# An mLSTM cell with a leaky-ReLU feed-forward block: the first product wholly in 64-row tiles, and the recurrent state updated in place

## The chip, the cores and the metric

The kernel runs on one core of one Trainium2 chip. The metric is the device time of one execution in microseconds (us). Three executions of the kernel before took 621.53, 621.92 and 622.60 us, median 621.92 us. The profile shown below is of one execution with a span of 621.0 us.

## What is computed

Each of 4 x 8 heads runs an mLSTM cell over 768 steps with head size 40. Its outputs are put side by side into rows of 320, and a two-layer block with a leaky ReLU follows.

```python
# q, k, v, o_gate: (4, 8, 768, 40);  i_gate, f_gate: (4, 8, 768)
for t in range(S):
    m_new = np.maximum(f_gate[:, :, t] + m, i_gate[:, :, t])
    f_stab = np.exp(f_gate[:, :, t] + m - m_new)
    i_stab = np.exp(i_gate[:, :, t] - m_new)
    C = f_stab * C + i_stab * outer(v_t, k_t)        # 40 x 40 a head
    n = f_stab * n + i_stab * k_t
    y[:, :, t] = sigmoid(o_t) * (C @ q_t) / max(|n . q_t|, 1)
x = y.transpose(0, 2, 1, 3).reshape(3072, 320)
h = x @ w_in                                          # 320 x 2048
out = np.maximum(0.01 * h, h) @ w_out                 # 2048 x 320
```

q, k, v and the gates are fp32. The two weight matrices come in as 64-bit floats, and the kernel turns them into fp32 itself.

## The kernel before

The sequence is cut into six chunks of 128 steps. A *cell* is one chunk of one of the four batches, so there are 24 cells; it is worked out in matrix form, with the state C (and n as its 41st column) carried from chunk to chunk. The four cells of a chunk give 512 rows of x, a *group*, and the feed-forward block runs on one group while the cells of the next chunk are worked out in between.

A cell goes through these steps, all named in the profile by the tiles they write. `u_transpose` transposes k and q (tkq, L311), and ScalarE copies them out (kqT, L314). `u_scores` makes the scores (sc, L323): two heads at a time, in the upper and lower half of TensorE's rows, since a head has 40 of 64 padded rows; VectorE multiplies them onto the mask w (L327). `u_state` multiplies the old state with q (pc, L337; VectorE scales it into hn, L341), makes the new contribution to the state (dC, L348), scales the old state on GpSimd (L357), and adds dC on VectorE (L358). The old and the new state lie in two tiles, C0 and C1, which swap from chunk to chunk. `u_values` multiplies w with v (pa, L367), VectorE adds it to hn (L369), forms the denominator, and `gate` makes x (VectorE L385, GpSimd L388). `u_x` transposes x (xt, L399 and L400), and ScalarE copies it into xT (L401, L403). `prep_mask`, `prep_exp`, `prep_vu` and `prep_o` prepare the next cell's mask (GpSimd L279, ScalarE L287), scaled values (GpSimd L295) and output gate (ScalarE L302).

The first product has 320 rows of w_in to contract: two full blocks of 128 and a rest of 64. For a pair of hidden blocks of 128, `full` runs two 128-row matmuls for each of the two blocks (L413), and `close` adds the rest of both in two 64-row matmuls (L419), one in each half of TensorE's rows, into two PSUM banks. For this xT holds the two full blocks, and the rest twice, once in each partition half. ScalarE then applies the leaky ReLU (act, L427). A pair is cut into two *units*: the first block, and the second block with the close. In the first group the pairs are run in halves of 256 columns (`half`, one unit each), so that the first two batches can start early. The second product runs in units of four hidden blocks (`part`, po, L457); ScalarE copies its result out (L462), and a transfer stores it.

Order of work: each engine takes its instructions in the order in which the program lists them (the program turns off reordering for TensorE, VectorE, ScalarE and GpSimd). `first_chunk` writes out by hand the order of the four cells of chunk 0, the first two half units and the conversion of the first weights. After it a loop goes over the units of the feed-forward block of one group and lets the units of the next chunk's cells in between, spread evenly. The conversion of a slice of weights (`narrow_weights`: one ScalarE and six VectorE instructions, L166 to L184) is likewise given out in pieces over the units of the first group. The transfers on SyncE's queue are placed by a planner.

PSUM has two pools of four banks: `mm` for ph (first product), po (second product) and the first masks, `c` for all tiles of the cells.

Of the kernel before, what the change touches and what calls it, by code (L numbers as in the profile page):

```python
# [9 lines left out]
F32 = mybir.dt.float32  # L10
# [3 lines left out]
ALU = mybir.AluOpType  # L14
# [4 lines left out]
def kernel(  # L19
# [26 lines left out]
    nc = tc.nc  # L46
    B, H, S, D = q.shape
    P = 128
    BH = B * H
    NB = S // P  # L50
    NS = B * NB
    Dm, FF = moe_w_in.shape
    PR = H // 2
    DP = 64
    D1 = D + 1
    NF = FF // P
    GT = B * P
    KF = Dm // P
    KR = Dm - KF * P
    assert NB * P == S and NF * P == FF and NF % 4 == 0 and D <= DP and H == 2 * PR and BH <= P  # L60
    assert KR == DP and GT * 4 <= 2048

    consts = ctx.enter_context(tc.tile_pool(name="consts", bufs=1))
    gp = ctx.enter_context(tc.tile_pool(name="gates", bufs=1))
    wk = ctx.enter_context(tc.tile_pool(name="wk", bufs=2))
# [38 lines left out]
        nc.gpsimd.memset(va_t[n][:, :, D:], 1.0)  # L104


    C_t = [consts.tile([P, B, PR, 2, D1], F32, name=f"C{n}") for n in range(2)]
    for t in C_t:
        nc.gpsimd.memset(t[:], 0.0)

    QN = NF // 4
    QC = 4 * P
    WC = KF * QC + 2 * P
    w_in = consts.tile([P, QN, WC], F32, name="w_in")
    w_out = consts.tile([P, NF, Dm], F32, name="w_out")

    def w_full(kk, f):
        n, e = divmod(f, 4)  # L120
        return w_in[:, n, kk * QC + e * P : kk * QC + (e + 1) * P]

    def w_rest(r, j):
        n, e = divmod(j, 2)
        return w_in[KR * r : KR * (r + 1), n, KF * QC + e * P : KF * QC + (e + 1) * P]

    wide = moe_w_in.dtype == U64
    raws = {}
# [1 line left out]
    def load_weights(n):  # L130

        if n < QN:
            dst = w_in[:, n, :]
        else:
            dst = w_out[:, 4 * (n - QN) : 4 * (n - QN + 1), :].rearrange("p a d -> p (a d)")
        to = dst
        if wide:
            raw = wk.tile([P, dst.shape[1]], U64, name="raw", bufs=3)
            raws[n] = (raw, dst)
            to = raw[:]  # L140
        if n < QN:
            cols = slice(n * QC, (n + 1) * QC)
            for kk in range(KF):
                nc.sync.dma_start(to[:, ts(kk, QC)], moe_w_in[ts(kk, P), cols])
            rest = moe_w_in[KF * P :, cols].rearrange("d (j two e) -> two d j e", two=2, e=P)
            for r in range(2):
                nc.sync.dma_start(
                    to[KR * r : KR * (r + 1), KF * QC :].rearrange("p (j e) -> p j e", e=P), rest[r],
                )
        else:  # L150
            rows = moe_w_out[(n - QN) * QC : (n - QN + 1) * QC, :]
            nc.sync.dma_start(to.rearrange("p (a d) -> p a d", d=Dm), rows.rearrange("(a p) d -> p a d", p=P))
# [40 lines left out]
    def gates(c):  # L193


        m0 = m0s.get(c)
        cs = ts(c, P)
        n = P if c == 0 else BH
        fc, il = (f0[:], i0[:]) if c == 0 else (f_sb[:, cs], i_sb[:, cs])
        F = wk.tile([n, P], F32, name="F", bufs=1)  # L200
        nc.vector.tensor_tensor_scan(F[:], fc, zeros[:n], 0.0, op0=ALU.add, op1=ALU.add)
        if c > 0:
            il_t = wk.tile([BH, P], F32, name="il", bufs=1)
            nc.vector.tensor_scalar(il_t[:], il, scalar1=m0[:], scalar2=None, op0=ALU.subtract)
            il = il_t[:]
        m = wk.tile([n, P], F32, name="m", bufs=1)
        nc.vector.tensor_tensor_scan(m[:], fc, il, -1e30 if c == 0 else 0.0, op0=ALU.add, op1=ALU.max)
        a = wk.tile([n, P], F32, name="a")
        nc.vector.tensor_tensor(a[:], F[:], m[:], op=ALU.subtract)
        if c > 0:  # L210
            nc.sync.dma_start(a_dr[c], a[:])
        bu = wk.tile([BH, 3, P], F32, name="bu")
        nc.vector.tensor_tensor(bu[:, 0, :], il[:BH], F[:BH], op=ALU.subtract)
        nc.scalar.activation(bu[:, 1, :], bu[:, 0, :], AF.Exp, bias=a[:BH, P - 1 :], scale=1.0)
        nc.scalar.activation(bu[:, 2, :], a[:BH], AF.Exp)
        if c + 1 < NB:
            m1 = wk.tile([BH, 1], F32, name="m0")
            if c == 0:
                nc.vector.tensor_copy(m1[:], m[:BH, P - 1 :])
            else:  # L220
                nc.vector.tensor_tensor(m1[:], m0[:], m[:, P - 1 :], op=ALU.add)
            m0s[c + 1] = m1
        return bu, a
# [105 lines left out]
    def u_state(s):  # L329
        c, b = divmod(s, B)  # L330
        d = st[s]
        C, C_new = C_t[c % 2], C_t[(c + 1) % 2]
        if c > 0:
            d["hn"] = wk.tile([P, H, D1], F32, name="hn")
            pc = psc.tile([P, H, D1], F32, name="pc", tag="c")
            for j in range(PR):
                nc.tensor.matmul(  # L337
                    pc[:, 2 * j : 2 * j + 2, :].rearrange("p h d -> p (h d)"), lhsT=d["kqT"][:, 1, j, :],
                    rhs=C[:, b, j].rearrange("p h d -> p (h d)"), start=True, stop=True,
                )  # L340
            nc.vector.tensor_tensor(  # L341
                d["hn"][:], pc[:], gT[:, c, 2, ts(b, H)].unsqueeze(2).to_broadcast([P, H, D1]), op=ALU.mult,
            )
        if c + 1 < NB:
            dC = psc.tile([P, PR, D1], F32, name="dC", tag="c")
            for h in range(H):
                rows = slice(DP * (h % 2), DP * (h % 2) + DP)
                nc.tensor.matmul(  # L348
                    dC[rows, h // 2, :], lhsT=d["kq"][:, 0, h, :], rhs=d["vu"][:, h, :], start=True, stop=True,
                )  # L350
            for r in range(2):
                rows = slice(DP * r, DP * r + DP)
                if c == 0:
                    nc.vector.tensor_copy(C_new[rows, b, :, r, :], dC[rows])
                else:
                    g = gL[rows, c, b * H + r : (b + 1) * H : 2].unsqueeze(2).to_broadcast([DP, PR, D1])
                    nc.gpsimd.tensor_tensor(C_new[rows, b, :, r, :], C[rows, b, :, r, :], g, op=ALU.mult)  # L357
                    nc.vector.tensor_tensor(C_new[rows, b, :, r, :], C_new[rows, b, :, r, :], dC[rows], op=ALU.add)  # L358

    def u_values(s):  # L360
        c, b = divmod(s, B)
# [28 lines left out]
    def u_x(s):  # L390

        c, b = divmod(s, B)
        d = st[s]
        if b == 0:
            st["xT", c] = wk.tile([P, KF + 1, GT], F32, name="xT")
        xT = st["xT", c]
        xt = psc.tile([P, KF + 1, P], F32, name="xt", tag="c")
        for kk in range(KF):
            nc.tensor.transpose(xt[:, kk, :], d["x"][:, ts(kk, P)], ident[:])  # L399
        nc.tensor.transpose(xt[:KR, KF, :], d["x"][:, KF * P :], ident[:])  # L400
        nc.scalar.copy(xT[:, :KF, ts(b, P)], xt[:, :KF, :])  # L401
        for r in range(2):
            nc.scalar.copy(xT[KR * r : KR * (r + 1), KF, ts(b, P)], xt[:KR, KF, :])  # L403
        del st[s]


    def ff_units(g):
        xT = st["xT", g]
        acts = {}

        def full(f, ph, cols):
            for kk in range(KF):
                nc.tensor.matmul(  # L413
                    ph[:, cols], lhsT=w_full(kk, f), rhs=xT[:, kk, cols], start=(kk == 0), stop=False,
                )

        def close(j, ph, cols):
            for r in range(2):
                nc.tensor.matmul(  # L419
                    ph[r][:, cols], lhsT=w_rest(r, j), rhs=xT[KR * r : KR * (r + 1), KF, cols],  # L420
                    start=False, stop=True,
                )
            for r in range(2):
                f = 2 * j + r
                if f not in acts:
                    acts[f] = wk.tile([P, GT], F32, name=f"act{f}", bufs=1)
                nc.scalar.activation(acts[f][:, cols], ph[r][:, cols], AF.Prelu, alpha=0.01)  # L427

        def pair(j):
            ph = {}  # L430

            def first():
                ph[0] = psf.tile([P, GT], F32, name="ph0", tag="mm")
                full(2 * j, ph[0], slice(0, GT))

            def second():
                ph[1] = psf.tile([P, GT], F32, name="ph1", tag="mm")
                full(2 * j + 1, ph[1], slice(0, GT))
                close(j, ph, slice(0, GT))

            return [first, second]

        def half(j, h):

            ph = [psf.tile([P, GT], F32, name=f"ph{r}", tag="mm") for r in range(2)]
            cols = ts(h, GT // 2)
            for r in range(2):
                full(2 * j + r, ph[r], cols)
            close(j, ph, cols)

        po = {}

# [201 lines left out]
```

## Time and profile before

| what | value |
|---|---|
| median of three executions | 621.92 us |
| TensorE matmuls (PE) busy | 597.4 us, 96% of the span |
| TensorE weight loads (PEld) busy | 385.7 us, 62% |
| VectorE (DVE) busy | 178.2 us, 29% |
| ScalarE (ACT) busy | 185.7 us, 30% |
| GpSimd (POOL) busy | 111.8 us, 18% |
| second product, L457 | 768 records, 221.4 us busy |
| first product, full tiles, L413 | 448 records, 186.2 us busy |
| first product, 64-row tiles, L419 | 224 records, 57.2 us busy |

How to read it: an fp32 matmul or weight load appears as two records, one for each pass. Matmuls are pipelined and their ends are modelled, so successive ones overlap in the list, and it is their starts that tell the pace. The form of a matmul on the array is written as rows*columns, 128*128 for the full array and 64*128 for a 64-row tile. Where a line of the timeline has [2.46 <-POOL x L388], the engine was idle for 2.46 us before it, until the named instruction released it.

### The profile page before, as it was taken

What the parts mean: (1) busy time and instruction counts of PE and PEld (TensorE: products, weight loads), DVE (VectorE), ACT (ScalarE), POOL (GpSimd) and SP (SyncE); (2) the same over time, 40 slices, a digit from 0 to 9 for tenths busy, and PEclk for the clock granted to TensorE, in tenths of its full rate; (3) what the DMA queues carried; (4) which work ended last, traced back from release to release, by engine and by line L of the source; (5) the groups of instructions that cost most, each with busy time, mean ns of one, the idle gap of its engine ahead of it and who ended that gap; (6) DMA issues with size and microseconds to landing.
All of it is one profiled execution on the core that took longest, in us unless ns stands there. A gap on an engine that the chain in (4) does not pass through costs nothing.

```text
span 621.0 us, 7722 instructions
## 1 busy us (share of the span) xinstructions
PE 597.4 (96%) x3046; PEld 385.7 (62%) x3046; DVE 178.2 (29%) x343; ACT 185.7 (30%) x493; POOL 111.8 (18%) x110
## 2 busy tenths in 40 slices
PE   6986998998999999999999999999999999999997
PEld 5865666776554577654577745577745567743575
DVE  5838656886221121311121411211101111100000
ACT  4442345332334403144403144223043231012100
POOL 3023021554202220302202302202101010000000
PEclk9997999999899999999999999999999999999999
DMA  9999434433221331312321313303300000000000
GB/s 180 226 234 217 147 97 130 91 73 67 67 51 36 76 77 28 81 23 65 77 51 48 78 24 74 77 13 86 77 11 1 1 0 22 11 12 0 0 22 21
DMA packets 111346, 41.50 MB, mean 67 GB/s; under 512 B 101104, under 2 KB 105616, under 8 KB 111312
## 3 DMA queue, kind: packets, MB, share of 16 engines
q1 hardware_dynamic: 111024, 40.79, 29.0%
q8 instruction: 24, 0.39, 0.3%
q10 hardware_dynamic: 288, 0.23, 0.2%
q14 instruction: 10, 0.08, 0.0%
HBM read 37.00 MB, written 4.01 MB: 66 GB/s over the span
## 4 chain that ended last, share of the span: by engine, by line
PE 87%; DVE 5%; SPq 3%; POOL 1%; ACT 1%; issue 1%; DMA 1%; POOLq 0%; DVEq 0%; ACTq 0%
PE po L457 32%; PE ph L413 27%; PE ph L419 8%; PE pa L367 6%; PE sc L323 4%; PE pc L337 3%; PE tkq L311 3%; SPq L242 2%; PE dC L348 2%; POOL x L388 1%; PE xt L399 1%; DMA va<-in_v_dram 1%; DVE hn L369 1%; DVE x L385 1%; DVE w_in L176 0%
## 5 line engine op out<-in xcount | busy, mean ns | idle before, releaser
L457 PE MATMUL po<-w_out,act 128*128 128x320 f32 x768 | 221.4, 440 | 0.0
L413 PE MATMUL ph<-xT,w_in 128*128 128x512 f32 (+1 forms) x448 | 186.2, 552 | 0.4 <-DVE w_in L184 0.4
L457 PEld LDWEIGHTS po<-w_out,act 128*128 128x128 f32 x768 | 142.3, 191 | 55.0 <-issue 1.9
L413 PEld LDWEIGHTS ph<-xT,w_in 128*128 128x128 f32 x448 | 81.5, 195 | 68.8 <-issue 58.5
L427 ACT ACTIVATE act<-ph 128x512 f32<-128x512 f32 (+1 forms) x112 | 53.7, 531 | 151.6 <-PE ph L419 151.6
L388 POOL TENSOR_TENSOR x<-x,den 128x320 f32<-128x320 f32 x24 | 22.9, 955 | 396.6 <-DVE x L385 396.6
L327 DVE TENSOR_TENSOR w<-w,sc 128x512 f32<-128x512 f32 x48 | 30.7, 681 | 182.3 <-PE sc L323 182.3
L287 ACT ACTIVATE w<-w,gT 128x128 f32<-128x128 f32 x192 | 58.7, 397 | 13.0 <-POOL w L279 12.8
L419 PE MATMUL ph<-xT,w_in 64*128 64x512 f32 (+1 forms) x224 | 57.2, 588 | 0.0
L462 ACT COPY y<-po 128x320 f32<-128x320 f32 x24 | 10.2, 424 | 148.5 <-PE po L457 86.6
L367 PEld LDWEIGHTS pa<-va,w 128*128 128x128 f32 x384 | 49.1, 203 | 8.5 <-issue 5.9
L279 POOL TENSOR_TENSOR w<-w,cmask 128x1024 f32<-128x1024 f32 x20 | 50.1, 2503 | 0.0
L367 PE MATMUL pa<-va,w 128*128 128x41 f32 x384 | 49.5, 291 | 0.4 <-DVE w L327 0.4
L314 ACT COPY kqT<-tkq 128x512 f32<-128x512 f32 x48 | 26.1, 593 | 75.2 <-PE tkq L311 75.1
L419 PEld LDWEIGHTS ph<-xT,w_in 64*128 64x128 f32 x224 | 17.3, 189 | 36.3 <-issue 36.3
L323 PEld LDWEIGHTS sc<-kqT 40*128 40x128 f32 x384 | 26.1, 204 | 12.8 <-issue 5.3
L323 PE MATMUL sc<-kqT 40*128 40x128 f32 x384 | 30.4, 302 | 1.7 <-ACT kqT L314 1.7
L369 DVE TENSOR_TENSOR hn<-hn,pa 128x328 f32<-128x328 f32 x20 | 9.9, 496 | 74.9 <-PE pa L367 74.9
L311 PEld LDWEIGHTS tkq<-ident,kq 128*128 128x128 f32 x192 | 23.7, 152 | 10.8 <-issue 9.4
L311 PE MATMUL tkq<-ident,kq 128*128 128x128 f32 x192 | 28.3, 295 | 0.0
L341 DVE TENSOR_TENSOR hn<-pc,gT 128x328 f32<-128x328 f32 x20 | 10.0, 498 | 60.6 <-PE pc L337 60.6
L337 PEld LDWEIGHTS pc<-C,kqT 128*128 128x128 f32 x160 | 20.6, 191 | 7.0 <-issue 5.3
(65 smaller groups left out, 316.8 us busy)
## 6 DMA issues: line engine op xcount, KB each, us to landing
w<-a_dr SPq DMA_DIRECT2D x20, 512.0 KB, 4.9
raw<-in_moe_w_out_dram SPq DMA_DIRECT2D x4, 1280.0 KB, 5.7
raw<-in_moe_w_in_dram SPq DMA_DIRECT2D x8, 512.0 KB, 5.5
kq<-in_k_dram SPq DMA_DIRECT2D x24, 160.0 KB, 3.1
kq<-in_q_dram SPq DMA_DIRECT2D x24, 160.0 KB, 3.5
va<-in_v_dram SPq DMA_DIRECT2D x24, 160.0 KB, 2.8
o_sb<-in_o_gate_dram SPq DMA_DIRECT2D x24, 160.0 KB, 4.7
out_dram<-y SPq DMA_DIRECT2D x24, 160.0 KB, 1.8
```

The lines of the kernel that those rows point to most:

```text
L279: nc.gpsimd.tensor_tensor(w[:], w[:], cmask[:].unsqueeze(1).to_broadcast([P, H, P]), op=ALU.add)
L287: nc.scalar.activation(w[:, h, :], w[:, h, :], AF.Exp, bias=gT[:, c, 0, bh : bh + 1], scale=1.0)
L311: nc.tensor.transpose(tp[:, j, :], d["kq"][:, i, 2 * j : 2 * j + 2, :].rearrange("p h d -> p (h d)"), ident[:],)
L323: nc.tensor.matmul(sc[r][:, j, :], lhsT=kqT[rows, 0, j, :], rhs=kqT[rows, 1, j, :], start=True, stop=True,)
L327: nc.vector.tensor_tensor(w[:, r::2, :], w[:, r::2, :], sc[r][:], op=ALU.mult)
L337: nc.tensor.matmul(pc[:, 2 * j : 2 * j + 2, :].rearrange("p h d -> p (h d)"), lhsT=d["kqT"][:, 1, j, :], rhs=C[:, b, j].rearrange("p h d - ...
L367: nc.tensor.matmul(pa[:, h, :], lhsT=d["w"][:, h, :], rhs=d["va"][:, h, :], start=True, stop=True)
L388: nc.gpsimd.tensor_tensor(x3, x3, d["den"][:].unsqueeze(2).to_broadcast([P, H, D]), op=ALU.mult)
L413: nc.tensor.matmul(ph[:, cols], lhsT=w_full(kk, f), rhs=xT[:, kk, cols], start=(kk == 0), stop=False,)
L419: nc.tensor.matmul(ph[r][:, cols], lhsT=w_rest(r, j), rhs=xT[KR * r : KR * (r + 1), KF, cols], start=False, stop=True,)
L427: nc.scalar.activation(acts[f][:, cols], ph[r][:, cols], AF.Prelu, alpha=0.01)
L457: nc.tensor.matmul(po[n][:], lhsT=acts[f][:, ts(n, P)], rhs=w_out[:, f, :], start=(f == 0), stop=(f == NF - 1),)
```

## The change

The whole first product is put into 64-row tiles. The 320 rows of w_in are five blocks of 64. For a pair of hidden blocks, one takes the upper half of TensorE's rows and the other the lower half: five steps, each of two 64-row matmuls side by side, one for each hidden block, into two banks. Thus no 128-row matmul is left in the first product, and TensorE's form doesn't change within it. Each half of the rows needs all five blocks of x on its own partitions, so xT now holds all of x on both partition halves. The five transposed blocks come out of the transposes on one half each, so the order of blocks differs between the halves (SLOTS), and the first copy still serves both; four smaller copies do the rest. w_in is laid out to match: two hidden blocks' weights for one half, two for the other, five blocks deep.

To make room, the second state tile goes (C is scaled and added to in place), and the small tiles a and bu have one buffer instead of two.

```diff
+    SLOTS = ([0, 2, 4, 1, 3], [1, 3, 0, 2, 4])
...
-    C_t = [consts.tile([P, B, PR, 2, D1], F32, name=f"C{n}") for n in range(2)]
-    for t in C_t:
-        nc.gpsimd.memset(t[:], 0.0)
+    C = consts.tile([P, B, PR, 2, D1], F32, name="C")
+    nc.gpsimd.memset(C[:], 0.0)
...
-            for kk in range(KF):
-                nc.sync.dma_start(to[:, ts(kk, QC)], moe_w_in[ts(kk, P), cols])
-            rest = moe_w_in[KF * P :, cols].rearrange("d (j two e) -> two d j e", two=2, e=P)
             for r in range(2):
...
+                while at < KC:
+                    ks = SLOTS[r][at:]
+                    n_k = next((i for i in range(1, len(ks)) if ks[i] != ks[i - 1] + 2), len(ks))
+                    nc.sync.dma_start(half[:, at : at + n_k, :], src[:, ks[0] : ks[0] + 2 * n_k - 1 : 2, :])
+                    at += n_k
...
-        a = wk.tile([n, P], F32, name="a")
+        a = wk.tile([n, P], F32, name="a", bufs=1)
-        bu = wk.tile([BH, 3, P], F32, name="bu")
+        bu = wk.tile([BH, 3, P], F32, name="bu", bufs=1)
...
-                    nc.gpsimd.tensor_tensor(C_new[rows, b, :, r, :], C[rows, b, :, r, :], g, op=ALU.mult)
-                    nc.vector.tensor_tensor(C_new[rows, b, :, r, :], C_new[rows, b, :, r, :], dC[rows], op=ALU.add)
+                    nc.gpsimd.tensor_tensor(C[rows, b, :, r, :], C[rows, b, :, r, :], g, op=ALU.mult)
+                    nc.vector.tensor_tensor(C[rows, b, :, r, :], C[rows, b, :, r, :], dC[rows], op=ALU.add)
...
-        nc.scalar.copy(xT[:, :KF, ts(b, P)], xt[:, :KF, :])
-        for r in range(2):
-            nc.scalar.copy(xT[KR * r : KR * (r + 1), KF, ts(b, P)], xt[:KR, KF, :])
+        nc.scalar.copy(xT[:, :KF, tok], xt[:, :KF, :])
+        nc.scalar.copy(xT[:DP, KF + 1 :, tok], xt[DP:, :KF, :])
+        nc.scalar.copy(xT[DP:, KF : 2 * KF, tok], xt[:DP, :KF, :])
+        nc.scalar.copy(xT[:DP, KF, tok], xt[:DP, KF, :])
+        nc.scalar.copy(xT[DP:, 2 * KF, tok], xt[:DP, KF, :])
...
-        def full(f, ph, cols):
-            for kk in range(KF):
-                nc.tensor.matmul(
-                    ph[:, cols], lhsT=w_full(kk, f), rhs=xT[:, kk, cols], start=(kk == 0), stop=False,
-                )
...
+        def rows(j, ph, cols, slots):
+            for slot in slots:
+                for r in range(2):
+                    nc.tensor.matmul(
+                        ph[r][:, cols], lhsT=w_row(r, slot, j), rhs=xT[DP * r : DP * (r + 1), slot, cols],
+                        start=(slot == 0), stop=(slot == KC - 1),
+                    )
...
             def first():
-                ph[0] = psf.tile([P, GT], F32, name="ph0", tag="mm")
-                full(2 * j, ph[0], slice(0, GT))
+                ph.extend(psf.tile([P, GT], F32, name=f"ph{r}", tag="mm") for r in range(2))
+                rows(j, ph, slice(0, GT), range(3))
 
             def second():
-                ph[1] = psf.tile([P, GT], F32, name="ph1", tag="mm")
-                full(2 * j + 1, ph[1], slice(0, GT))
-                close(j, ph, slice(0, GT))
+                rows(j, ph, slice(0, GT), range(3, KC))
+                relu(j, ph, slice(0, GT))
```

More of the change, by code (lines that the diff above doesn't have):

```diff
@@ L59 @@
     KR = Dm - KF * P
+    KC = Dm // DP
+    SLOTS = ([0, 2, 4, 1, 3], [1, 3, 0, 2, 4])
     assert NB * P == S and NF * P == FF and NF % 4 == 0 and D <= DP and H == 2 * PR and BH <= P
-    assert KR == DP and GT * 4 <= 2048
+    assert KR == DP and KC == 5 and KC * DP == Dm and GT * 4 <= 2048
     consts = ctx.enter_context(tc.tile_pool(name="consts", bufs=1))
@@ L104, with f_of, w_row @@
         nc.gpsimd.memset(va_t[n][:, :, D:], 1.0)
-    C_t = [consts.tile([P, B, PR, 2, D1], F32, name=f"C{n}") for n in range(2)]
-    for t in C_t:
-        nc.gpsimd.memset(t[:], 0.0)
+    C = consts.tile([P, B, PR, 2, D1], F32, name="C")
+    nc.gpsimd.memset(C[:], 0.0)
     QN = NF // 4
     QC = 4 * P
-    WC = KF * QC + 2 * P
+    WC = KC * 2 * P
     w_in = consts.tile([P, QN, WC], F32, name="w_in")
     w_out = consts.tile([P, NF, Dm], F32, name="w_out")
[L119 to L123, printed above, removed]
+    def f_of(r, j):
         n, e = divmod(j, 2)
-        return w_in[KR * r : KR * (r + 1), n, KF * QC + e * P : KF * QC + (e + 1) * P]
+        return 4 * n + 2 * r + e
+    def w_row(r, slot, j):
+        n, e = divmod(j, 2)
+        at = (2 * slot + e) * P
+        return w_in[DP * r : DP * (r + 1), n, at : at + P]
     wide = moe_w_in.dtype == U64
@@ L141, in load_weights @@
         if n < QN:
-            cols = slice(n * QC, (n + 1) * QC)
-            for kk in range(KF):
-                nc.sync.dma_start(to[:, ts(kk, QC)], moe_w_in[ts(kk, P), cols])
-            rest = moe_w_in[KF * P :, cols].rearrange("d (j two e) -> two d j e", two=2, e=P)
             for r in range(2):
-                nc.sync.dma_start(
-                    to[KR * r : KR * (r + 1), KF * QC :].rearrange("p (j e) -> p j e", e=P), rest[r],
-                )
+                cols = slice(n * QC + 2 * P * r, n * QC + 2 * P * (r + 1))
+                src = moe_w_in[:, cols].rearrange("(k p) c -> p k c", p=DP)
+                half = to[DP * r : DP * (r + 1), :].rearrange("p (k c) -> p k c", k=KC)
+                at = 0
+                while at < KC:
[3 more added lines that the diff above has]
+                    at += n_k
         else:
@@ L331, in u_state @@
         d = st[s]
-        C, C_new = C_t[c % 2], C_t[(c + 1) % 2]
         if c > 0:
@@ L353, in u_state @@
                 if c == 0:
-                    nc.vector.tensor_copy(C_new[rows, b, :, r, :], dC[rows])
+                    nc.vector.tensor_copy(C[rows, b, :, r, :], dC[rows])
                 else:
                     g = gL[rows, c, b * H + r : (b + 1) * H : 2].unsqueeze(2).to_broadcast([DP, PR, D1])
-                    nc.gpsimd.tensor_tensor(C_new[rows, b, :, r, :], C[rows, b, :, r, :], g, op=ALU.mult)
-                    nc.vector.tensor_tensor(C_new[rows, b, :, r, :], C_new[rows, b, :, r, :], dC[rows], op=ALU.add)
+                    nc.gpsimd.tensor_tensor(C[rows, b, :, r, :], C[rows, b, :, r, :], g, op=ALU.mult)
+                    nc.vector.tensor_tensor(C[rows, b, :, r, :], C[rows, b, :, r, :], dC[rows], op=ALU.add)
     def u_values(s):
@@ L394, in u_x @@
         if b == 0:
-            st["xT", c] = wk.tile([P, KF + 1, GT], F32, name="xT")
+            st["xT", c] = wk.tile([P, KC, GT], F32, name="xT")
         xT = st["xT", c]
@@ L400, in u_x @@
         nc.tensor.transpose(xt[:KR, KF, :], d["x"][:, KF * P :], ident[:])
-        nc.scalar.copy(xT[:, :KF, ts(b, P)], xt[:, :KF, :])
-        for r in range(2):
-            nc.scalar.copy(xT[KR * r : KR * (r + 1), KF, ts(b, P)], xt[:KR, KF, :])
+        tok = ts(b, P)
+        nc.scalar.copy(xT[:, :KF, tok], xt[:, :KF, :])
[3 more added lines that the diff above has]
+        nc.scalar.copy(xT[DP:, 2 * KF, tok], xt[:DP, KF, :])
         del st[s]
@@ L409, in ff_units, with relu @@
         acts = {}
-        def full(f, ph, cols):
-            for kk in range(KF):
-                nc.tensor.matmul(
-                    ph[:, cols], lhsT=w_full(kk, f), rhs=xT[:, kk, cols], start=(kk == 0), stop=False,
-                )
-        def close(j, ph, cols):
-            for r in range(2):
[L419 to L424, printed above, removed]
+        def rows(j, ph, cols, slots):
[5 more added lines that the diff above has]
+                    )
+        def relu(j, ph, cols):
+            for r in range(2):
+                f = f_of(r, j)
                 if f not in acts:
@@ L429, in pair @@
         def pair(j):
-            ph = {}
+            ph = []
             def first():
-                ph[0] = psf.tile([P, GT], F32, name="ph0", tag="mm")
-                full(2 * j, ph[0], slice(0, GT))
+                ph.extend(psf.tile([P, GT], F32, name=f"ph{r}", tag="mm") for r in range(2))
+                rows(j, ph, slice(0, GT), range(3))
             def second():
-                ph[1] = psf.tile([P, GT], F32, name="ph1", tag="mm")
-                full(2 * j + 1, ph[1], slice(0, GT))
-                close(j, ph, slice(0, GT))
+                rows(j, ph, slice(0, GT), range(3, KC))
+                relu(j, ph, slice(0, GT))
             return [first, second]
@@ L446, in half @@
             cols = ts(h, GT // 2)
-            for r in range(2):
-                full(2 * j + r, ph[r], cols)
-            close(j, ph, cols)
+            rows(j, ph, cols, range(KC))
+            relu(j, ph, cols)
         po = {}
```

## The prediction

> **What bounds the kernel now.** I read the busy shares first, then the chain of work that ended last:
>
> ```profile
> PE 597.4 (96%) x3046; PEld 385.7 (62%) x3046; DVE 178.2 (29%) x343; ACT 185.7 (30%) x493; POOL 111.8 (18%) x110
> ...
> PE 87%; DVE 5%; SPq 3%; POOL 1%; ACT 1%; issue 1%; DMA 1%; POOLq 0%; DVEq 0%; ACTq 0%
> ```
>
> TensorE (PE) is busy for 96% of the span and makes up 87% of the chain. All that its instructions waited for from 160 us to the end, in the view of waits, is:
>
> ```profile
> PE xt L399 <- POOL x L388: 1.0, 4, 0.3
> ```
>
> So after 160 us only what TensorE does back to back counts. Before 160 us it had 23.6 us without a running matmul (60 + 60 + 80 us less 45.6 + 57.9 + 77.1 busy), and there the other engines count too.
>
> A busy TensorE is not a streaming TensorE. The timeline of the last group, which has no cell work in it (columns: start us, duration us, what):
>
> ```profile
> 545.66 3.60 PE L413 MATMUL ph<-xT,w_in 128*128 128x512 f32 x8
> 549.18 1.13 PE L419 MATMUL ph<-xT,w_in 64*128 64x512 f32 x4
> 550.25 3.70 PE L413 MATMUL ph<-xT,w_in 128*128 128x512 f32 x8
> 553.88 1.13 PE L419 MATMUL ph<-xT,w_in 64*128 64x512 f32 x4
> 554.93 3.70 PE L413 MATMUL ph<-xT,w_in 128*128 128x512 f32 x8
> ```
>
> An fp32 matmul shows as two passes, so x8 is four full matmuls, and x4 is two 64-row matmuls that run side by side as two pass times. Starts count, since the ends are modelled and overlap. One round lasts 554.93 - 550.25 = 4.68 us. What should a pass cost? The weight loads of a full stream tell:
>
> ```profile
> 401.49 0.19 PEld L413 LDWEIGHTS ph<-xT,w_in 128*128 128x128 f32 x1 [0.24 <-issue]
> 401.92 0.19 PEld L413 LDWEIGHTS ph<-xT,w_in 128*128 128x128 f32 x1 [0.24 <-issue]
> ```
>
> They come every 0.43 us, each beside a running pass. The round is 8 + 2 = 10 pass times, 4.29 us at 0.429. The other 0.39 us is the price of going into the 64-row form and back: about 0.20 us per change of form. It splits. Eight full passes take 549.18 - 545.66 = 3.52 us when full tiles precede, and 553.88 - 550.25 = 3.63 us after a 64-row tile: about 0.10 us is the first weight load, which nothing covers. The rest of 0.20 (3.52 less 8 x 0.429 is 0.09) is the array running empty before the form changes.
>
> **What the Trainium skill says.** "TensorEngine Tiling (Array Packing)", Key Properties: changing the tiling mode, not just the tile, drains TensorE; tiles of one mode work independently. The trace agrees: 0.09 us ahead of the first 64-row pass, and scores (L323) that run in pairs. "TensorE: Matmul & The Clock Gate", The mechanism: a weight load overlaps running matmuls only when the row group differs. Read strictly that would leave loads of one tile exposed; the full stream above has each load beside a pass, so here the measurement decides. Its part on the HAM clock gate says that the clock falls to half after about 3.4 us without work. The trace half agrees: after an idle 2.46 us before 155.16 the granted clock averaged 0.66 over 155 to 160 us, that is 3.4 us at half, or 1.7 us lost; after 1.66 us it stayed:
>
> ```profile
> 90.00:100.00 10.00, 8.34 (x64) 6.43 (x66) 7.11 (x13) 6.50 (x20) 0.00 (x0) 1.00 0.50 149
> 155.00:160.00 5.00, 4.84 (x14) 3.31 (x15) 3.84 (x5) 1.19 (x4) 4.17 (x5) 0.66 0.46 125
> ...
> 94.99 1.23 PE L323 MATMUL sc<-kqT 40*128 40x128 f32 x16 [1.66 <-ACT kqT L314]
> 155.16 0.44 PE L399 MATMUL xt<-ident,x 128*128 128x128 f32 x2 [2.46 <-POOL x L388]
> ```
>
> **The change part by part.** *Streaming.* A pair of hidden blocks was 8 full passes and 2 paired ones; it becomes 10 paired ones. The work in passes is the same, if a long run of pairs keeps 0.429 us a pass. Two places of the trace bear on that:
>
> ```profile
> 192.74 1.13 PE L419 MATMUL ph<-xT,w_in 64*128 64x512 f32 x4
> 193.70 1.06 PE L323 MATMUL sc<-kqT 40*128 40x128 f32 x16
> ...
> 34.16 2.08 PE L323 MATMUL sc<-kqT 40*128 40x128 f32 x16
> 36.17 0.69 PE L399 MATMUL xt<-ident,x 128*128 128x128 f32 x2
> ```
>
> A closing pair followed by scores, also in 64-row form, takes 193.70 - 192.74 = 0.96 us: 0.53 for the first pass with its bare load, 0.43 for the second, nothing for a change. Eight score pairs of 128 columns at the half clock take 2.01 us, of which 8 x 0.213 = 1.71 is streaming and about 0.3 the change at both ends: no extra per pair. So I take 0.429. Bounds: 0.429 and 0.53 (each load bare). The weight loads grow from 6 to 10 fp32 loads a pair, two at a time, each hidden under a pass.
>
> *Changes of form.* I counted them in the order in which TensorE receives its instructions (the column-tiled dC counts as a form too): 200 before, 155 after. By group of 512 tokens: 64 to 41 in the first, 32 to 30 in each of the next three, 24 to 22 in the fifth, 16 to 2 in the last. A change between long matmuls costs 0.20 us. Beside cell work it costs less: starts in the trace give 0.12 before or after pa, 0.16 before tkq or pc, 0.13 before xt, because those are short and their loads were never wholly hidden. In a middle group 13 changes go (8 into the closing pair, 2 back to full tiles, 1 to scores, 2 from scores), 13 x 0.20 = 2.6 us, and 11 come (po to ph, three tkq to ph and one xt to ph at 0.20; two pa to ph at 0.12; one more each to tkq, pc, pa, xt, 0.57 together), 1.8 us. Net 0.8 us, four times: 3.1 us. Last group: 14 x 0.20 = 2.8 us, all on the path.
>
> *First group.* Its 23 fewer changes are worth 4.6 us by the same prices, but not all is on the path. The first two half units (from 38 us) feed a stretch that ends in TensorE waiting 4.98 us for x at 57.8 us: nothing gained. The eight half units from 59.2 us to the gate transposes at 81.7 us run back to back: 15 changes, 3.0 us. From there to the scores at 95.0 us TensorE waits: masks' exp on ScalarE, w_out's conversion and the next gates on VectorE and then kqT make a chain of 13.3 us that does not shrink; the idle 1.66 us before those scores grows to about 3. Then two more halves save 0.6 us. So 3.6 us, less a possible half-clock spell after the longer gap, 0 or 1.7 us; I take the middle, 0.8.
>
> *ScalarE.* Per cell, two 64 x 256 copies more:
>
> ```profile
> 34.27 0.37 ACT L401 COPY xT<-xt 128x256 f32<-128x256 f32 x1 [3.24 <-PE xt L400]
> 34.54 0.53 ACT L403 COPY xT<-xt 64x128 f32<-64x128 f32 x2
> ```
>
> By the spacing, 0.27 to 0.37 us each, so 0.55 to 0.74 us a cell, 13 to 18 us in all on an engine that is 30% busy. Queued behind are a mask's exp, a prelu or kqT. The first matmul of a group follows the last transposes of x by 24 matmul records of po (253.55 to 260.01 us): hidden. In the first group the first half unit starts some 0.4 us later, inside the slack before 57.8 us. The prelu of a pair is due a whole pair (4.3 us) later, since four banks hold two pairs: hidden.
>
> *State in place.* GpSimd's scaling (L357, two of 0.58 us, up to 2.25 us together beside VectorE) now waits for pc's matmuls to have read C; before it ran ahead. VectorE's two adds follow it, about 1 us later than now; behind them stands hn += pa, which waits for matmuls at least one unit (1.7 us) later. TensorE wants dC's bank two allocations on. Cost: 0, at most 0.6 us a cell, 20 cells. One memset (1.19 us) goes from idle GpSimd: 0.
>
> *Loads and buffers.* w_in moves the same bytes in as many transfers, 2 KB rows instead of 4 KB and 1 KB. ScalarE never waited for w_in's landing: 0. One buffer for a and bu: the first a is read by matmuls whose results VectorE uses before the next gates; each later one by a transfer a group earlier: 0.
>
> Sum: 3.1 + 2.8 + 3.6 - 0.8 = 8.7 us; 621.9 - 8.7 = **613.2 us**.
>
> **Rivals.** *The start keeps its time*: the gain before 160 us is eaten by ScalarE and VectorE there and a half-clock spell comes on top: 621.9 - 5.9 = 616.0, or 617.7. For it: the waits before 160 us. Against: eight halves stand in a row without a wait. *Loads are bare in the paired stream*: 0.104 us on each of 400 passes, 41.6 us, and some 10 in the first group: about 665 us, slower. For it: the only in-pair step of L419 is 0.53 us. Against: it follows a change; the scores show none. *New waits take the place*: 0.65 us for each of 20 cells by the later state and copies, 13 us: 626 us, slower. For it: both are in the cell's own path. Against: 1.0 us of waits after 160 us, with units of 1.7 us and more between the steps.
>
> **How the numbers follow.** Forecast 0.75, start keeps its time 0.16, bare loads 0.04, new waits 0.05. The range 610 to 617.5 takes in first-group gains from nothing to 5 us, with or without a half-clock spell, and leaves out the two slower cases and the far end of the first rival. Faster 0.75 + 0.16 less a little for part of the new waits: 0.90; same 0.02; slower 0.08.
>
> **What would show it.** Right: in the last group a stream of 64-row passes every 0.429 us, 8 rounds from 545.66 to 583.08 (37.4 us) becoming 34.6 us; 96.3 us from 163.70 to 260.01 becoming 95.5; the wait for kqT before the first scores of the second chunk at about 3 us. Wrong: passes further apart than 0.44 us, new TensorE waits for ScalarE's xT or act after 160 us, GpSimd's C ending after the next pa, or a long half-clock stretch.

## The result, and the profile after

The changed kernel takes 615.36 us (median, 614.92 to 615.85) beside 622.26 us (621.53 to 622.95): the ratio is 0.989, 95% interval 0.9876 to 0.9904, or 6.9 us less. Measured again later (e8), it took 615.07 us beside 622.69 us, ratio 0.988 (0.9863 to 0.9896). The forecast was 613.2 us with a range of 610.0 to 617.5.

The profiled span fell by 7.5 us, from 621.0 to 613.5 us. The busy shares and the chain of work, in the page of the changed kernel:

```profile
PE 584.0 (95%) x3494; PEld 390.2 (64%) x3494; DVE 177.1 (29%) x343; ACT 206.1 (34%) x541; POOL 107.4 (18%) x109
PE 79%; SPq 7%; DVE 4%; DMA 3%; ACT 3%; POOL 2%; issue 2%; POOLq 0%; DVEq 0%; ACTq 0%
```

TensorE has 448 records more (1120 in the first product for 672), and is busy for 13.4 us less. ScalarE is busy for 20.4 us more: the five copies per cell into xT, where three were, make 17.5 us of it (38.8 for 21.3). What is not TensorE's in the chain lies before 160 us, where it now follows transfers (SPq, DMA); no engine shows a wait for the landing of w_in, so the page alone does not say that they cost time. All that TensorE waited for after 160 us, in the view of waits:

```profile
PE xt L402 <- POOL x L391: 0.9, 4, 0.3
```

It is the same short wait as before (1.0 us), so no new one came up behind 160 us. The last group's first product, eight pairs, in the timeline (start us, duration us):

```profile
541.03 34.60 PE L420 MATMUL ph<-xT,w_in 64*128 64x512 f32 x160
575.57 1.61 PE L457 MATMUL po<-w_out,act 128*128 128x320 f32 x5
```

From 541.03 to 575.57 it takes 34.54 us, where it took 37.42 us (545.66 to 583.08). The weight loads in that stream:

```profile
541.03 0.30 PEld L420 LDWEIGHTS ph<-xT,w_in 64*128 64x128 f32 x4 [0.44 <-issue]
541.57 0.19 PEld L420 LDWEIGHTS ph<-xT,w_in 64*128 64x128 f32 x2 [0.23 <-issue]
542.00 0.19 PEld L420 LDWEIGHTS ph<-xT,w_in 64*128 64x128 f32 x2 [0.24 <-issue]
542.43 0.19 PEld L420 LDWEIGHTS ph<-xT,w_in 64*128 64x128 f32 x2 [0.24 <-issue]
```

Loads now come two at a time, one for each half of the rows, every 0.43 us: the pace of a pass is what it was in full tiles. Only the first step, from 541.03 to 541.57, is longer by the bare load.

Where the 7.5 us came from, by the starts of the groups' first products in both timelines:

| stretch (from one profile each) | before, us | after, us | gain, us | forecast, us |
|---|---|---|---|---|
| to the second group's first product | 163.70 | 161.74 | 1.96 | 2.8 |
| second to fourth group, each | 96.31 | 95.67 | 0.64 | 0.8 |
| fifth group | 93.01 | 92.28 | 0.73 | 0.8 |
| last group's first product | 37.42 | 34.54 | 2.88 | 2.8 |

Behind the first group these times come again within 0.03 us in every profile of the same code; the first row does not, as the experiments show.

### The profile page after: what moved, and what is told of

Its sections match the earlier page's. It is cut to its first block, busy times and chain, and to the rows that moved or that the text cites. A ratio compares the mean times of both kernels' runs of the same rounds, so it can differ in the third digit from the quotient of the medians.

```text
span 613.5 us, 8662 instructions
## 1 busy us (share of the span) xinstructions
PE 584.0 (95%) x3494; PEld 390.2 (64%) x3494; DVE 177.1 (29%) x343; ACT 206.1 (34%) x541; POOL 107.4 (18%) x109
## 4 chain that ended last, share of the span: by engine, by line
PE 79%; SPq 7%; DVE 4%; DMA 3%; ACT 3%; POOL 2%; issue 2%; POOLq 0%; DVEq 0%; ACTq 0%
PE po L457 31%; PE ph L420 30%; PE pa L370 6%; SPq L246 4%; PE sc L327 3%; PE pc L340 3%; PE tkq L315 3%; SPq L152 2%; PE dC L351 2%; DMA va<-in_v_dram 1%; DMA raw<-in_moe_w_in_dram 1%; PE xt L402 1%; ACT w L291 1%; POOL w L283 1%; POOL x L391 1%
## 5 line engine op out<-in xcount | busy, mean ns | idle before, releaser
L420 PE MATMUL ph<-xT,w_in 64*128 64x512 f32 (+1 forms) x1120 | 224.1, 546 | 1.1 <-ACT xT L405 0.6
L420 PEld LDWEIGHTS ph<-xT,w_in 64*128 64x128 f32 x1120 | 107.1, 192 | 85.4 <-issue 78.3
L370 PEld LDWEIGHTS pa<-va,w 128*128 128x128 f32 x384 | 48.8, 202 | 13.4 <-issue 6.7
L360 POOL TENSOR_TENSOR C<-C,gL 64x164 f32<-64x164 f32 x32 | 14.8, 462 | 184.9 <-PE pc L340 183.7
L327 PE MATMUL sc<-kqT 40*128 40x128 f32 x384 | 28.1, 287 | 2.7 <-ACT kqT L318 2.7
L299 POOL TENSOR_TENSOR vu<-va,gT 128x328 f32<-128x328 f32 x20 | 18.8, 941 | 28.0 <-issue 18.8
```

The lines of the kernel that those rows point to most:

```text
L327: nc.tensor.matmul(sc[r][:, j, :], lhsT=kqT[rows, 0, j, :], rhs=kqT[rows, 1, j, :], start=True, stop=True,)
L370: nc.tensor.matmul(pa[:, h, :], lhsT=d["w"][:, h, :], rhs=d["va"][:, h, :], start=True, stop=True)
L420: nc.tensor.matmul(ph[r][:, cols], lhsT=w_row(r, slot, j), rhs=xT[DP * r : DP * (r + 1), slot, cols], start=(slot == 0), stop=(slot == KC ...
```

## The experiments

### The state alone (e1)

```diff
-    C_t = [consts.tile([P, B, PR, 2, D1], F32, name=f"C{n}") for n in range(2)]
...
+    C = consts.tile([P, B, PR, 2, D1], F32, name="C")
...
-        a = wk.tile([n, P], F32, name="a")
+        a = wk.tile([n, P], F32, name="a", bufs=1)
...
-                    nc.gpsimd.tensor_tensor(C_new[rows, b, :, r, :], C[rows, b, :, r, :], g, op=ALU.mult)
...
+                    nc.gpsimd.tensor_tensor(C[rows, b, :, r, :], C[rows, b, :, r, :], g, op=ALU.mult)
...
```

> The kernel before with only the state updated in place and one buffer for a and bu; the first product as before. My theory (the wait of GpSimd for pc is hidden): 621.9 us, within 0.5 us of the kernel before, and no new TensorE wait. Rival (the later state costs part of the gain): 2 to 12 us slower, with VectorE's adds or pa later in every cell.

Measured: 622.61 beside 622.37 us, ratio 1.0003 (0.9994 to 1.0012). The later scaling of the state is hidden, and the rival falls. One part of the expectation was not met: the profile has TensorE waits of 4.5 us together before pa, all ahead of 160 us, where the profile before has 0.4. They are not the state's, since e9, with both state tiles, shows 4.4 us of them.

### The copies alone (e2)

```diff
+        x2 = wk.tile([P, KF, P], F32, name="x2", bufs=1)
+        nc.scalar.copy(x2[:DP], xt[DP:, :KF, :])
+        nc.scalar.copy(x2[DP:], xt[:DP, :KF, :])
```

> The kernel before with two more 64 x 256 copies of the transposed x per cell on ScalarE, into a tile that nothing reads. My theory: hidden but for the first group, where the bank is given back later: two waits of dC of about 0.3 us, so 0 to 0.8 us slower than the kernel before. Rival (ScalarE's copies hold TensorE up in every group): 24 cells by 0.5 us, some 12 us slower.

Measured: 623.94 beside 622.37 us, ratio 1.0026 (1.0017 to 1.0034), or 1.6 us slower (1.1 to 2.1). This is far from 12 us, and more than my 0 to 0.8. Two places show in its timeline:

```profile
38.62 3.78 PE L416 MATMUL ph<-xT,w_in 128*128 128x256 f32 x8 [0.52 <-ACT xT L401]
58.28 0.69 PE L399 MATMUL xt<-ident,x 128*128 128x128 f32 x2 [4.97 <-POOL x L388]
...
115.97 0.67 PE L348 MATMUL dC<-vu,kq 128*64 128x41 f32 x16 [0.17 <-ACT x L406]
```

The first half unit begins 0.6 us later (38.62 for 38.02), because the second cell's first copy stands behind the first cell's additional ones and the eight exp of a mask. The transposes at 57.83 then come at 58.28, and the wait ahead of them is 4.97 us as before. So this wait is no slack: x, which it waits for, comes itself from that first half unit, by way of ScalarE's prelu, copies and weight conversion and VectorE's part of that conversion, all of which come 0.4 to 0.5 us later in the timelines. Second, dC waits for the bank that x's transposes held. Together they make some 0.8 us in this one profile; the second group starts 0.7 us later (164.41 for 163.70), and the groups behind it take the same time as before. The other half of the 1.6 us I could not place.

### Forcing changes of form (e3) and a control (e4)

```diff
                         start=(slot == 0), stop=(slot == KC - 1),
                     )
+                if g == NB - 1:
+                    tn = psc.tile([P, P], F32, name="tn", tag="c")
+                    nc.tensor.matmul(
+                        tn[:, :32], lhsT=ident[:P, :], rhs=zeros[:P, :32], start=True, stop=True,
+                    )
```

The control has `ident[:DP, :]` and `zeros[:DP, :32]`, which makes it a matmul in a 64-row tile.

> The changed kernel with a tiny full-array matmul (32 columns, its result unused) after each of the 40 steps of the last group's first product, so that the form changes twice per step. If a change of form costs 0.20 us: 40 x (0.40 + 0.05 for the matmul itself), the last group's first product 18 us longer than 34.5 us. If the gain had another cause (the weight loads of 64-row tiles hide better than those of full tiles) and the change of form is nearly free: 40 x 0.1 = 4 us longer, as with the tiny matmul in 64-row form.

> The control: the same 40 tiny matmuls in the form of a 64-row tile, so that the form never changes. Change of form as cause: 40 x 0.05 to 0.11 us, 2 to 4.5 us longer than the changed kernel. If any interruption of the paired stream costs (one half idle, bare loads): up to 18 us, as with the full-array ones.

Measured: 636.68 us and 624.94 us. The timeline of the last group with full-array matmuls in between:

```profile
540.51 1.13 PE L420 MATMUL ph<-xT,w_in 64*128 64x512 f32 x4
541.57 0.41 PE L426 MATMUL tn<-zeros,ident 128*128 128x32 f32 x2
541.91 1.13 PE L420 MATMUL ph<-xT,w_in 64*128 64x512 f32 x4
```

and the same place in the control:

```profile
542.29 0.19 PE L426 MATMUL tn<-zeros,ident 64*128 64x32 f32 x1
542.30 0.69 PE L420 MATMUL ph<-xT,w_in 64*128 64x512 f32 x1
542.32 0.27 PE L426 MATMUL tn<-zeros,ident 64*128 64x32 f32 x1
542.43 1.10 PE L420 MATMUL ph<-xT,w_in 64*128 64x512 f32 x3
543.37 0.19 PE L426 MATMUL tn<-zeros,ident 64*128 64x32 f32 x1
```

A step of two passes, 0.86 us in the undisturbed stream, takes 1.40 us with the full-array matmul (541.91 - 540.51), 0.54 more, and 1.08 us in the control (543.37 - 542.29), 0.22 more. Over the 40 steps the first product's stretch grows from 34.54 us to 55.81 and 43.38 us. Both estimates were too low: I expected 0.45 and at most 0.11 a step. The starts in the control suggest why. The tiny matmul stands in the upper half alone, and the loads behind it lie bare in both halves in turn, which would make the 0.22 us without any change of form. What remains for the two changes of form is 0.54 - 0.22 = 0.32 us. If the full-array case pays as much for the interruption as the control does, 0.16 us a change is a lower bound, and 0.20 us with the bare load counted in, as the prediction counted it, fits between this and 0.27 (half of 0.54, which has the tiny matmul in it).

### One half after the other (e5)

```diff
-            for slot in slots:
-                for r in range(2):
+            for r in range(2):
+                for slot in slots:
```

> The changed kernel with the two halves one after the other: in each unit all matmuls of the upper half first, then all of the lower half. If the two 64-row tiles run side by side only when their matmuls alternate in the instruction order: ten more pass times a pair, 8 pairs x 4.29 us = 34 us more in the last group, some 200 us in all. If each half had a queue of its own that looks past the other's: no change.

Measured: 668.55 us, ratio 1.0738 to the kernel before (1.0691 to 1.0785). Neither expectation is met. The last group and a part of the second group of its timeline:

```profile
590.17 35.57 PE L420 MATMUL ph<-xT,w_in 64*128 64x512 f32 x160
625.67 0.54 PE L457 MATMUL po<-w_out,act 128*128 128x320 f32 x1
...
199.07 1.99 PE L420 MATMUL ph<-xT,w_in 64*128 64x512 f32 x8
201.00 1.98 PE L370 MATMUL pa<-va,w 128*128 128x41 f32 x16
202.91 3.81 PE L420 MATMUL ph<-xT,w_in 64*128 64x512 f32 x12
206.64 1.09 PE L315 MATMUL tkq<-ident,kq 128*128 128x128 f32 x8
```

The last group takes 35.50 us, one more than with alternating halves, and not 34 more: the lower half's matmuls overtake queued ones of the upper half. The trace does not name the half of a record, but a second row of starts sets in 0.97 us after the first, about two passes, and both then advance every 0.43 us. In this long stream the delay is paid once. In the middle groups, where cell steps cut the first product, the group takes 103.05 us for 95.67, 7.4 us more, and not every cut pays. A unit of three steps (x12, three matmuls of one half listed ahead of the other half's) takes 3.73 us (202.91 to 206.64) for 2.78 (180.69 to 183.47 in the changed kernel). A unit of two steps (x8) takes 1.93 us (199.07 to 201.00) for 1.92 (176.86 to 178.78), so there both halves run together in spite of the order. Two matmuls listed ahead are passed, with three the first has to end. The rest of the loss, some 20 us, is in the first group. There five matmuls of a half stand ahead, and the delay is paid in each half unit: three of them without a cut take 9.38 us (97.79 to 107.17) for 6.67 (80.02 to 86.69 in the changed kernel). In this profile half clock also lasts longer (passes of 256 columns start only every 0.43 us until 77 us, every 0.22 us behind it); how the 20 us divide was not worked out. So alternating the halves is worth having, but not because the order in the list is the order on the array.

### Fewer changes of form by another way (e6)

The cells of the third to sixth chunk are placed by hand. `plan` says after which unit of a group (0 to 15 first product, 16 to 31 second) a cell step comes:

```diff
+                put(1 + 4 * b, u_scores, s0 + b)
+                put(16 + 2 * b, u_state, s0 + b)
+                put(17 + 2 * b, value, s0 + b)
+                put(25 if b == 3 else 19 + 2 * b, u_x, s0 + b)
...
+                    put(25 + b, u_transpose, s0 + B + b)
...
-        d["kqT"] = wk.tile([P, 2, PR, P], F32, name="kqT")
+        d["kqT"] = wk.tile([P, 2, PR, P], F32, name="kqT", bufs=NL)
...
-            raw = wk.tile([P, dst.shape[1]], U64, name="raw", bufs=3)
+            raw = wk.tile([P, dst.shape[1]], U64, name="raw", bufs=2)
```

> The changed kernel with the cells of the third to sixth chunk placed anew: the scores (64-row form) among the first product's units, everything else of a cell among the second product's, so that TensorE changes its form 83 times in place of 155. kqT gets four buffers, the raw weights two. Change of form as cause, by the prices of the prediction: 25.2 less 13.7 = 11.5 us less, about 604 us. Rival (form changes are not what bounds the middle groups, and the denser cells in the second product's units wait for one another): no gain or a loss, 615 us or more, with TensorE waits for VectorE and GpSimd.

Measured: 600.71 us beside 622.69 us, ratio 0.9648 (0.9634 to 0.9662). Counted in its trace, with the last transpose of x (written 128*64) taken as a full tile as in the prediction, TensorE changes its form 83 times for 155. It beats both kernels: 22.0 us less than before, and 14.4 us less than the changed kernel on the same chip (615.07). A part of its second group:

```profile
180.35 8.75 PE L420 MATMUL ph<-xT,w_in 64*128 64x512 f32 x40
188.93 1.06 PE L327 MATMUL sc<-kqT 40*128 40x128 f32 x16
189.83 8.75 PE L420 MATMUL ph<-xT,w_in 64*128 64x512 f32 x40
```

Between 40 records of the first product and the next 40 there are only the scores, which have the same form; they take 0.90 us (188.93 to 189.83), eight steps of 0.112. There is no TensorE wait after 160 us in its view of waits. 72 changes less gave 14.4 us, 0.20 us each; but 0.9 us of it are the waits for x that are gone, and without them it is 0.19. I had expected 11.5 us from the lower prices of the prediction for changes beside pa, pc, xt and tkq. Some of those prices were too low, as shown below; the 72 changes were not worked out one by one.

### ScalarE's copies first (e7), and the changed kernel again (e8)

```diff
-                    if fn is u_transpose:
+                    if fn is u_transpose and s % B == 0:
                         ahead(s + 1)
+                    elif fn is u_x and s % B < B - 1:
+                        ahead(s + 2)
```

> The changed kernel with the preparation of the next mask listed after the transposes of x, so that ScalarE's copies into xT no longer stand behind the eight exp. If dC's two waits in the first group come from that order: they vanish, 0.6 us less than the changed kernel (about 614.8 us). If they do not matter or the mask becomes late: 615.4 us or more, with scores or pa waiting.

> The changed kernel itself on the same chip, as the mark for the other three: 615.4 us.

Measured: 615.57 us (ratio 0.9887, 0.9872 to 0.9902) and 615.07 us (0.988, 0.9863 to 0.9896). dC's two waits of 0.29 us are gone from the view of waits, but the time is not less. With intervals of about 1 us on each side 0.6 us could not have been told for certain. In the profile TensorE's idle 2.66 us ahead of the scores, the same gap as in the changed kernel, was followed by half clock here:

```profile
90.84 1.23 PE L327 MATMUL sc<-kqT 40*128 40x128 f32 x16 [2.66 <-ACT kqT L318]
91.84 3.88 PE L420 MATMUL ph<-xT,w_in 64*128 64x256 f32 x20
```

Twenty records of 256 columns take 3.88 us there, for 2.43 us at full clock (85.75 in the same timeline). The window of 90 to 100 us has a granted clock of 0.83 (the third number from the end):

```profile
90.00:100.00 10.00, 9.16 (x82) 7.87 (x82) 5.65 (x9) 6.04 (x17) 0.92 (x2) 0.83 0.58 165
```

and in the first profile of the changed kernel, after the same gap:

```profile
90.00:100.00 10.00, 7.34 (x82) 6.36 (x80) 7.25 (x13) 7.23 (x20) 0.92 (x2) 1.00 0.58 166
```

The spell does not come from the new order: e3, with the changed kernel's own first group, has 0.83 in the same window after the same gap. So dC's waits came from the order of the copies, as supposed, but what they cost (0.58 us) is smaller than what such a spell takes (1.45 us). In the runs with profiles whose first group is the changed kernel's own, the second group's first product begins at 161.74, 160.53 (again), 161.21 (e3) and 162.03 us (e4): 1.5 us of spread, all of it in the first group.

### The placement of e6 in full tiles (e9), and with the copies first (e10)

e9 is the kernel before with the diff of e6; e10 is e6 with the diff of e7.

> The kernel before, with its full tiles, and only the new placement of the cells from the grouped run: 174 changes of form in place of 200. At 0.20 us each: 5.2 us less than the kernel before, about 617 us, and 91 changes (some 18 us) more than the grouped run in 64-row tiles at 600.7 us. Rival (the placement alone made that gain, by shorter waits): about 607 us, 14 us less than the kernel before.

> The grouped run with ScalarE's copies ahead of the exp in the first group. If dC's two waits and nothing else are at stake: 0 to 0.6 us less than the grouped run, about 600.4 us. If the earlier arrival only lengthens the wait before the first scores of the second chunk and brings a half-clock spell there: 600.7 us or up to 1 us more.

Measured: e9 614.74 us beside 621.56 us, ratio 0.9891 (0.9873 to 0.9908), 6.8 us less (5.7 to 7.9): a little over the 5.2 us that 26 fewer changes should give, and far from the 14 us of the rival. Here too 1.0 us of waits for x is gone, which leaves 5.8 us, 0.22 us a change. The placement gains 14.4 us only when the first product is in 64-row tiles as well, because only then do its scores meet their own form. e10 600.55 us, ratio 0.9661 (0.9646 to 0.9675): as e6, and a difference of 0.6 us could not be told. In its profile the wait before the scores of the second chunk is 3.1 us for 2.7, and the granted clock over 90 to 100 us is 0.83 for 1.00, as the second expectation has it. Between e9 and e10, on one chip, lie 14.2 us, where 91 changes were expected to make some 18: 0.16 us a change, or 0.17 with the 1.6 us that the copies of 64-row tiles cost (e2).

## Why the prediction was right, point by point

The forecast held in its mechanism, the changes of form, and it was too high in the first group and a little in the middle groups. The 615.36 us lie nearer to the 616.0 us of the rival that the start keeps its time than to 613.2 us, so the time alone does not part the two; the trace does, and only in part.

**The pace of a pass.** It was taken as 0.429 us in a long run of pairs. It is: 0.43 us in the loads of the last group, and 34.54 us for eight pairs where 34.6 was forecast. The rival of bare loads falls.

**The price of a change of form.** 0.20 us between long matmuls. The last group: 14 changes, 2.88 us, 0.21 each. e6: 72 changes, 0.19 to 0.20 each. e9: 26 changes, 0.22 to 0.26. e3 against e4 points to 0.16 us or more.

**Changes beside short cell work.** These were priced at 0.12 us before or after pa, 0.16 beside pc and 0.13 beside xt. The price of the way out of pa was right, the ways in were priced too low, and that term of the sum was too small. The profile before shows it already:

```profile
180.37 1.13 PE L419 MATMUL ph<-xT,w_in 64*128 64x512 f32 x4
181.43 1.98 PE L367 MATMUL pa<-va,w 128*128 128x41 f32 x16
183.24 1.96 PE L413 MATMUL ph<-xT,w_in 128*128 128x512 f32 x4
185.04 1.04 PE L311 MATMUL tkq<-ident,kq 128*128 128x128 f32 x8
...
202.85 1.88 PE L367 MATMUL pa<-va,w 128*128 128x41 f32 x16
204.55 1.96 PE L413 MATMUL ph<-xT,w_in 128*128 128x512 f32 x4
```

Behind 64-row tiles pa's block lasts 1.81 us (181.43 to 183.24), between full tiles 1.70 us (202.85 to 204.55). The 0.1 us between them is the first weight load, which is bare. The pair ahead of it lasts 1.06 us (180.37 to 181.43), 0.20 over its two passes: 0.10 for its own bare load, and 0.10 in which no load and no matmul starts. So the change into pa costs 0.20 us, where 0.12 was taken. The same sums give 0.20 us into pc, and 0.15 into xt and tkq (taken at 0.13 and 0.16). Out of pa, in the profile after:

```profile
176.86 1.99 PE L420 MATMUL ph<-xT,w_in 64*128 64x512 f32 x8
178.78 1.98 PE L370 MATMUL pa<-va,w 128*128 128x41 f32 x16
180.69 2.85 PE L420 MATMUL ph<-xT,w_in 64*128 64x512 f32 x12
183.47 1.09 PE L315 MATMUL tkq<-ident,kq 128*128 128x128 f32 x8
```

The block lasts 1.91 us (178.78 to 180.69), 0.10 more than on the way into full tiles. The first load behind it costs 0.10 us (2.78 us for six passes, another 0.10 being the change into tkq), but in full tiles it cost 0.08 as well (1.80 us for four passes from 183.24). That makes 0.12 us, as taken. The changes "one more each to tkq, pc, pa, xt", taken at 0.57 us together, come to some 0.7, and turn the forecast 0.8 us a middle group into 0.65; measured was 0.64. This cost the forecast some 0.6 us over four groups.

**The first group.** 3.6 us less half a clock spell was forecast, 2.8 us. The two profiles of the changed kernel have 1.96 and 3.17 us against the one profile before; but here a single profile is unsure by more than 1 us: in that of e1, which is as fast as the kernel before, the second group starts at 162.43 us. The medians are surer. All that lies behind gave 5.5 us in each profile (the table without its first row), so of 6.9 and 7.6 us the first group gave 1.4 and 2.1. The chain of ScalarE and VectorE from the gate transposes to the second chunk's first scores is as long as before (79.49 to 92.81 us, 13.32 us for 13.31), as the prediction said, and the wait ahead of those scores grew from 1.66 to 2.66 us. The eight half units gained. Before:

```profile
59.18 3.78 PE L413 MATMUL ph<-xT,w_in 128*128 128x256 f32 x8 [0.45 <-DVE w_in L184]
...
81.68 0.37 PE L228 MATMUL tg<-ident,bu 32*128 32x32 f32 x3
```

and after:

```profile
59.60 19.96 PE L420 MATMUL ph<-xT,w_in 64*128 64x256 f32 x160 [0.45 <-DVE w_in L188]
79.49 0.37 PE L232 MATMUL tg<-ident,bu 32*128 32x32 f32 x3
```

That is 22.50 and 19.89 us, 2.6 us of the 3.0 forecast, with a granted clock over 60 to 65 us of 0.65 before and 0.55 after. The stretch starts 0.42 us later. The step that failed is the one about ScalarE: "the first half unit starts some 0.4 us later, inside the slack before 57.8 us". There was no slack. x at 57.8 us hangs on that half unit, and e2 shows the whole 0.45 us coming through.

**The copies elsewhere.** They were called hidden: true after 160 us, not in the first group, where "TensorE wants dC's bank two allocations on" was counted for the state only. The same rotation gives dC the bank of x's transposes, which the five copies now hold longer: two waits of 0.29 us. e2 puts the copies at 1.6 us in all (1.1 to 2.1), of which 0.8 is accounted for; behind the first group its profile shows no difference.

**The state in place, loads and buffers.** 0 was forecast and e1 measured -0.4 to 0.7 us for state and buffers. In the changed kernel's second group VectorE's last add to C ends at 177.78 us, 1.0 us before the next pa. The new layout of w_in was not tried by itself.

Of the forecast 8.7 us, 6.9 and 7.6 us came: 5.5 of 5.9 from the groups behind the first, and 1.4 and 2.1 of 2.8 from the first. The copies' 1.6 us are enough to cover what is missing there, but the clock spells of the first group were not held fixed in any run, so its account stays open by about 1 us.

Two sums of the prediction are off, and nothing hangs on them. TensorE was without a running matmul for 19.4 us before 160 us, not 23.6 (200 less 45.6, 57.9 and 77.1). And the range's lower end by its own terms is 611 us (621.9 less 5.9 and 5), not 610.

## What to carry to other kernels

When TensorE is busy throughout and waits for nobody, look at the starts of its instructions: the work in passes was the same before and after, and the gain lay in the 0.1 to 0.2 us that each change between full and 64-row form costs. Count the changes in the instruction order before rewriting anything. Putting work of one form next to its own kind gave 6.8 us alone, as much as the change did, but 14.4 us on top of it, since only both together let the scores meet their own form. And a wait that looks like slack has to be followed back before anything is hidden in it.

## What the runs showed of the hardware that was not expected

Matmuls of one half of the rows overtake queued ones of the other: with the halves listed one after the other (e5) the last group took 35.50 us for 34.54. The look-ahead was short: with two matmuls of one half listed ahead the other half started with it (1.93 us for 1.92), with three it started 0.97 us later. The Trainium skill, "TensorE: Matmul & The Clock Gate", The mechanism, says that matmuls start and end in strict order; for two row tiles this trace differs: the second half started 0.97 us behind the first, though three matmuls, six passes of 0.43 us, stood ahead of it in the list. And a tiny matmul in one half of a paired stream costs 0.22 us (e4), four times the 0.054 us that its two passes of 32 columns take at the pace of the others (0.429 us for 512).
